# Attention values on four 64x64 array tiles, shared PSUM banks and a new instruction order in a fused attention and gated-MLP kernel

## The chip, the cores and the metric

The kernel runs on one core of one Trainium2 chip. The metric is the device time of one execution in microseconds; the median of several runs is compared, and a change is told from no change by runs of both kernels on the same chip. The core has five engines with queues of their own: TensorE (PE in the profile, with its weight loads as PEld), VectorE (DVE), ScalarE (ACT), GpSimd (POOL) and SyncE (SP, which here only issues DMAs). Every engine works off its own queue in order and waits on semaphores for the others.

## The reference

The input is an attention over short chunks, followed by a gated MLP. There are 4 batches, 8 heads, 768 positions and 64 dimensions a head.

```python
for c in range(nc):                       # 24 chunks of 32 queries
    l_start = max(0, c_start - 16); r_end = min(S, c_end + 8)
    k_full = concat([mem_k, k[l_start:r_end]])     # 8 + up to 56 keys = 64
    scores = scale * q_c @ k_full.T
    a = exp(scores - max(scores)); a = a / (sum(a) + 1e-9)
    out[c_start:c_end] = a @ v_full
x = out, heads side by side: (4, 768, 512)
h = gelu(x @ w_in); u, v = halves of h             # 512 and 512 wide
v_n = layer_norm(v) * g_ln
v_s = einsum('ts,bsd->btd', w_sg, v_n) + b_sg
y = x + (u * v_s) @ w_out
```

## The kernel before

The work is cut into 24 units `u` of 128 queries (4 batches `b`, 6 tiles `tt`), each with four chunks `c` and eight heads. A unit goes through these steps (`attention_steps`, L291), named with the unit's number:

- `q`, `k`, `v`: DMAs of the inputs, two, two and three buffers deep.
- `S`: 32 matmuls on tiles of 64 rows by 32 columns into two PSUM banks `s` (L159); the profile shows two records for each matmul in float32.
- `mx`, `sb`: DVE takes the largest score and subtracts it; `ex`: ACT's exponential; `z`: a few zeros by POOL; `sm`: DVE's sum, plus 1e-9, and reciprocal, three instructions in one step; `nm`: the product with it, on DVE or POOL.
- The weights must then lie with the keys on the partitions. Units 0 to 9 (`PAIRS = 10`) use TensorE: `T` transposes into the bank `t`, and `pa` and `pb` copy the two halves of partitions into `pt_all`. Units 10 to 23 use DVE and DMA: `yt` transposes blocks of 32x32, and `E`, once for two units, issues 16 DMAs of 32 KB from `y_t` to `pt_all`.
- `A`: the values (L382). Two heads share a matmul: 128 rows hold the keys of both heads, and `pt_all` keeps zeros in the other head's half, so that one matmul of 128 rows, 64 columns and 64 moving columns gives both. There are 16 matmuls, 32 records, into a bank `av` (L161).
- `xc`, `xh`, `xl`: copy of the result, its high part, and the low part (result minus high part), which the MLP multiplies as three products high x low, low x high and high x high.

The MLP is written in steps as well: `V` + batch + tile is the product for the gate half with 12 matmuls of 512 columns, followed by the gelu (`v1` to `v4`), the statistics (`v5`, three instructions), `v6` (POOL), `v7`, and `v8` and `v9` for the high and low parts. `U` + batch + half + block is the other half, with 12 matmuls of 384 columns, and `u1` to `u4`. `W` is the product over the sequence with 18 matmuls, and `w1` to `w4`; `O` is the last product with 12, `o1` adds the residual and `out` stores. The weights come as 64-bit floats and are taken apart by `d1` to `d9` (`weight_steps`, L199) and, for `w_sg`, by `ga` and `gb`; `cb` and `cbh` bring the two vectors. `zz6` stands for six warm matmuls of the identity that compute nothing needed. The products of the MLP and the warm matmuls write into a pool of four PSUM banks `mm` (L158); together with `s`, `t` and `av` all eight are taken.

What runs when is written out by hand: `ORDER` lists all steps in program order, and `InOrder` (L95) keeps each engine's instructions in that order. A step that can run on two engines has a star where the second one is taken (`nm0*` is on POOL, `d7i10*` on DVE). So the list is the queue of every engine, read by picking out its steps. Since every instruction passes through the helper `InOrder`, nearly all rows of the profile carry its line, L103, and are told apart by their tiles. Accesses to one PSUM tile by different engines are ordered bank by bank: an instruction that writes a bank waits for all earlier ones, in program order, that read that bank of the tile, and the other way round.

Of the kernel before, what the change touches and what calls it, by code (L numbers as in the profile page):

```python
# [39 lines left out]
d4i01 d5i00 d7i02* d2i03 d8i02 d1i03 d4i03 d2o0 d9i02* d3i03 nm1 d4o0 d5i03 T1 v100 d6o0 pa1 cbh v200 pb1  # L40
sb3 A1 v300 ex3 v400 T2 sm3 v4 xc1 d7i00 S4 pa2 v500 xh1 k6 nm3* pb2 mx4 q6 d8i00 A2 sb4 v600 ex4 S5 xl1* v5
xh2 T3 d9i00 sm4 q7 xc2 V01 k7 pa3 mx5 pb3 nm4 sb5 xl2 ex5 d6i03 S6 z5 v101 d6i01 A3 k8 mx6 q8 V02 d7i03* v6
xc3 v201 d8i03 d1i01 xh3 d9i03* v301 xl3* d3i01 v401 T4 V03 d5i01 pb4 v501 d7i01 pa4 sb6 v601 v700 d8i01 sm5
ex6 A4 v800 d9i01* z6 v701 S7 ga20 v7 nm5* sm6 ga50 U001 k9 ga41 mx7 xh4 q9 v900 ga00 xl4 v801 xc4 T5 gb20*
v103 U002 nm6 g11 pb5 gb00* pa5 v203 v901 g21 ga40 sb7 ga30 T6 v303 gb50* A5 ex7 gb40 v403 g10 pa6 sm7 S8
ga11 v8 gb41 xc5 V04 v503 g51 xh5 k10 gb11 mx8 ga21 q10 u1002 xl5 v603 g01 ga10 u2002 nm7* pb6 sb8 v102 A6
u3002 v202 gb10 ex8 u4002 S9 ga51 v9 sm8 gb30 xc6 U010 g31 v302 mx9 k11 gb51 u1001 q11 v402 ga01 u2001 gb01
v502 V05 u3001 u1010 v703 v602 u2010 v803 v702 u3010 gb21* v802 u4010 v903 ga31 T7 u4001 U012 pa7 pb7* v902
v105 sb9 v205 ex9 gb31 A7 v104 sm9 v305 v204 S10 u1012 v10 xc7 nm9 U003 k12 v304 v405 q12 u2012 mx10 u3012
v404 U000 u1003 u4012 v504 u2003 v604 U013 v505 u3003 u1000 u4003 v605 u2000 v704 u3000 U011 v705 v804 u4000  # L50
v805 v904* v905* d1o0 W002 nm8 d3o0 d5o0 ro1 d7o0 d8o0 T8 w1002 W003 d9o0 pa8 sb10 pb8* ex10 w2002 sm10
w3002 d1o1 d2o1 S11 d3o1 w4002* d4o1 W001 d5o1 k13 u1013 nm10 q13 d6o1 u2013 ro2 d7o1 mx11 u3013 w1003 A8
d8o1 u4013 w1001 W000 w2003 v11 xc8 w2001 w3003 d9o1* w3001 d2o2 d1o2 d4o2 w4001 d3o2 W013 d6o2 u1011 u2011
w4003 w1000 u3011 d5o2 w2000 ro3 d7o2 u4011 w3000 W012 w1013 d8o2 w4000* w2013 d9o2* w3013 w4013* d1o3 W010
d2o3 d3o3 w1012 d4o3 d5o3 w2012 d6o3 w3012 yt10 w4012 W011 w1010 d7o3 w2010 w3010 d8o3 w4010* d9o3 T9 w1011
pa9 sb11 O000 pb9 w2011 ex11 w3011 z11 sm11 O002 w4011* nm11* o1000 out000 O001 o1002 yt11 out002 O011 o1001
out001 O010 o1011 out011 O012 o1010 out010 O013 o1012 out012 O003 o1013 out013 S12 o1003 xh6 A9 xh7 out003
xl6* xh8 k14 mx12 V10 q14 xl7* E5 xl8* sb12 xc9 ex12 xh9 V12 z12 sm12 v110 xl9 v210 nm12* v310 v410 V11 v112
v510 v12 v212 v610 v312 v710 v412 v810 V13 v910 v512 yt12 v612 v111 v712 v211 v812 A10 v311 v912 U100 v411
v13 xc10 xh10 v511 v113 xl10 v213 A11 u1100 v611 v313 u2100 V14 v711 v14 xc11 v413 u3100 xh11 u4100 v811  # L60
v513 xl11 U101 v613 v911 v713 v114 V15 u1101 v214 v813 u2101 v314 v913 u3101 v414 u4101 U102 v514 v115 v215
v614 v714 v315 U103 v814 v415 u1102 v914 v515 u2102 v615 U110 u3102 u1103 v715 u4102 v815 u2103 v915 u3103
U111 u1110 u4103 u2110 u3110 u4110 W100 u1111 u2111 u3111 u4111 W101 w1100 w2100 w3100 w4100 W102 w1101
w2101 w3101 w4101 W103 w1102 w2102 w3102 w4102 U112 w1103 w2103 w3103 w4103 U113 u1112 u2112 u3112 u4112 S13
# [5 lines left out]
xl14 yt17 A15 o1112 out112 O113 xc15 E8 V20 o1113 xh15 xl15 V21 v120 v220 v18 out113 v320 v420 V22 v520 v121  # L70
v221 v620 v321 v720 v421 v820 A16 v920 v521 V23 v621 v19 xc16 v122 v721 xh16 v222 v821 xl16 v322 v422 A17
v921 v522 V24 v20 xc17 v622 v123 v722 xh17 v223 v822 xl17 v323 U200 v423 v922 v523 v124 v623 V25 v224 u1200
v723 v324 u2200 v823 v424 u3200 v923 v524 U201 u4200 v624 v125 v724 v225 v824 U202 v325 v924 u1201 v425
u2201 v525 u3201 U203 u1202 u4201 v625 u2202 v725 u3202 v825 u4202 U210 u1203 v925 u2203 u3203 u4203 W200
u1210 u2210 u3210 u4210 W201 w1200 w2200 w3200 w4200 W202 w1201 w2201 w3201 w4201 W203 w1202 w2202 w3202
w4202 U211 w1203 w2203 w3203 w4203 U212 u1211 u2211 u3211 u4211 S18 u1212 U213 u2212 k20 mx18 u3212 q20
u4212 sb18 W210 ex18 u1213 z18 sm18 u2213 nm18 u3213 u4213 S19 yt18 W211 w1210 k21 q21 mx19 w2210 sb19 w3210
w4210 ex19 sm19 W212 w1211 nm19 w2211 yt19 w3211 w4211 E9 S20 w1212 W213 w2212 mx20 w3212 w4212 sb20 ex20
sm20 S21 w1213 O200 nm20 mx21 k22 w2213 q22 sb21 w3213 k23 O201 q23 w4213 ex21 o1200 out200 sm21 nm21 A18
yt20 o1201 O202 v21 xc18 yt21 out201 A19 o1202 out202 O203 E10 xc19 S22 o1203 xh18 O210 xh19 xl18 mx22 sb22  # L80
xl19 ex22 S23 sm22 O211 out203 o1210 v22 mx23 out210 nm22 sb23 O212 o1211 ex23 out211 z23 yt22 sm23 A20
o1212 nm23 O213 out212 xc20 v23 yt23 xh20 xl20 A21 o1213 out213 V30 E11 xc21 xh21 xl21 V31 v130 v230 v330
v430 V32 v530 v131 v231 v630 v331 v730 v431 v830 V33 v930 v531 v631 v132 v731 v232 v831 A22 v332 v931 v432
U300 xc22 v532 v133 xh22 v233 v632 xl22 v333 A23 u1300 v433 U301 v732 xc23 v533 v832 xh23 u2300 v932 u3300
V34 u1301 u4300 xl23 u2301 u3301 v633 u4301 v733 V35 v833 v134 v933 v234 v334 v434 U302 v135 v534 v235 v634
v335 v734 U303 u1302 v435 v834 u2302 v934 v535 u3302 U310 u4302 u1303 v635 u2303 v735 u3303 v835 u4303 U311
u1310 v935 u2310 u3310 u4310 W300 u1311 u2311 u3311 u4311 W301 w1300 w2300 w3300 w4300 W302 w1301 w2301
w3301 w4301 W303 w1302 w2302 w3302 w4302 U312 w1303 w2303 w3303 w4303 U313 u1312 u2312 u3312 u4312 W310
u1313 u2313 u3313 u4313 W311 w1310 w2310 w3310 w4310 W312 w1311 w2311 w3311 w4311 W313 w1312 w2312 w3312
# [512 lines left out]
```

## Time and profile before

| | us |
|---|---|
| median of 3 runs | 420.61 |
| lowest, highest | 416.58, 421.05 |
| the profiled execution's own time | 422.26 |
| its span in the profile | 420.5 |

| engine | busy us | share of the span |
|---|---|---|
| PE | 378.9 | 90% |
| PEld | 346.8 | 82% |
| DVE | 283.5 | 67% |
| ACT | 166.8 | 40% |
| POOL | 130.2 | 31% |

The mean granted TensorE clock of the span is 0.971 of the full one. A busy engine is one that has an instruction in it. PE's matmuls are pipelined and their ends are modelled, so the time of a burst is best read from its first start to the next burst's first start. A row of the timeline gives start, length, engine, line, operation, tiles written and read, shape and count; a row of the waits gives total, count and longest.

### The profile page before, as it was taken

Reading aid. Unit: us, or ns where it says so; the run is one execution under the profiler, and the core shown is the slowest. Engines: PE = TensorE matmul, PEld = TensorE weight load, DVE = VectorE, ACT = ScalarE, POOL = GpSimd, SP = SyncE. Lnnn points to the kernel's source line nnn. Section 1 sums busy time; section 2 is a strip of 40 time slices with the busy share of each in tenths; the row PEclk is TensorE's granted clock in tenths of the full one; section 3 lists DMA queues with packets and bytes.
Section 4 is the critical chain, followed back from the end, with each engine's and each line's share of the span. In section 5 each row is a group of like instructions: output and inputs, shape, how many; then the busy total and the mean of one; then the engine's idle time right before and its main releaser. Section 6 shows DMA issues by size and latency. Waiting matters only on the chain. (4 is left out here: it accounts for less than half of the span.)

```text
span 420.5 us, 9642 instructions
## 1 busy us (share of the span) xinstructions
PE 378.9 (90%) x4026; PEld 346.8 (82%) x4026; DVE 283.5 (67%) x536; ACT 166.8 (40%) x307; POOL 130.2 (31%) x136
## 2 busy tenths in 40 slices
PE   3663998899989998999998979999989899999996
PEld 3652787699989977999986858999978888999996
DVE  5999799998994477845764555844973567753332
ACT  4545678654450236613222235623222246533100
POOL 3433346712331045421202225422111125422210
PEclk9996799999999999999999898999998999999999
DMA  8992656532412423001162924001227350000012
GB/s 289 397 388 94 223 161 206 195 112 82 133 50 76 142 89 107 2 0 63 36 222 55 320 71 146 2 0 62 64 50 246 101 160 21 2 0 2 0 64 88
DMA packets 24523, 47.56 MB, mean 113 GB/s; under 512 B 4384, under 2 KB 13600, under 8 KB 24480
## 3 DMA queue, kind: packets, MB, share of 16 engines
q1 hardware_dynamic: 24480, 46.94, 33.8%
q8 instruction: 32, 0.52, 0.5%
q14 instruction: 11, 0.09, 0.1%
HBM read 36.96 MB, written 6.29 MB: 103 GB/s over the span
## 5 line engine op out<-in xcount | busy, mean ns | idle before, releaser
L103 PE MATMUL s<-ka,qa 64*32 64x64 f32 x768 | 11.0, 238 | 8.1 <-DMA qa<-in_qs 5.7
L103 PEld LDWEIGHTS s<-ka,qa 64*32 64x32 f32 x768 | 9.0, 112 | 10.9 <-DMA ka<-in_ks 6.0
L103 PEld LDWEIGHTS av<-pt,vb 128*64 128x64 f32 x256 | 9.9, 156 | 7.8 <-issue 4.2
L103 PE MATMUL av<-pt,vb 128*64 128x64 f32 x256 | 11.5, 246 | 4.5 <-DMA pt<-y 2.4
L103 PEld LDWEIGHTS av<-pt,vc 128*64 128x64 f32 x256 | 9.2, 148 | 7.5 <-issue 5.9
L103 PE MATMUL av<-pt,vc 128*64 128x64 f32 x256 | 10.7, 237 | 4.9 <-DMA pt<-y 3.8
L103 ACT ACTIVATE eb<-eb 128x512 f32<-128x512 f32 x12 | 7.6, 630 | 18.2 <-DVE eb L103 17.8
L103 DVE STREAM_TRANSPOSE y<-ea 128x512 f32<-128x512 f32 x7 | 5.0, 710 | 13.6 <-DMA pt<-y 13.6
L103 PEld LDWEIGHTS av<-pt,va 128*64 128x64 f32 x256 | 8.4, 137 | 6.1 <-issue 3.9
L103 PE MATMUL av<-pt,va 128*64 128x64 f32 x256 | 9.7, 226 | 4.1 <-DMA pt<-y 2.9
L103 DVE SCALAR_TENSOR_TENSOR gb<-gb,mmd 128x512 f32<-128x512 f32 x12 | 8.2, 680 | 7.2 <-ACT gb L103 7.2
L103 ACT ACTIVATE ga<-ga 128x512 f32<-128x512 f32 (+1 forms) x14 | 8.8, 632 | 9.7 <-DVE ga L103 9.7
L103 ACT COPY pt<-t 64x512 f32<-64x512 f32 x18 | 10.4, 579 | 4.4 <-PE t L103 4.2
L103 PE MATMUL s<-kb,qb 64*32 64x64 f32 x768 | 10.7, 231 | 1.6 <-DVE ea L103 1.4
L103 PEld LDWEIGHTS s<-kb,qb 64*32 64x32 f32 x768 | 8.7, 109 | 3.9 <-DVE ea L103 1.8
L103 ACT COPY xa<-av 128x512 f32<-128x512 f32 x9 | 5.2, 583 | 16.1 <-PE av L103 14.1
L103 ACT ACTIVATE gb<-gb 128x512 f32<-128x512 f32 (+1 forms) x14 | 8.9, 635 | 5.8 <-DVE gb L103 5.7
L103 PE MATMUL mma<-ident 128*128 128x128 f32 x50 | 9.6, 356 | 1.4 <-POOL ident masks.py:199 1.4
L103 ACT ACTIVATE ea<-ea 128x512 f32<-128x512 f32 x12 | 7.6, 632 | 7.3 <-DVE ea L103 7.3
L103 DVE SCALAR_TENSOR_TENSOR gb<-gb,mmc 128x512 f32<-128x512 f32 x8 | 5.4, 678 | 7.4 <-ACT gb L103 7.4
L103 DVE SCALAR_TENSOR_TENSOR mma<-mma,g_half,b_half 128x384 f32<-128x384 f32 x9 | 5.5, 613 | 7.2 <-PE mma L103 7.2
L103 PEld LDWEIGHTS mma<-ident 128*128 128x128 f32 x50 | 8.5, 257 | 1.8 <-POOL ident masks.py:199 1.4
(501 smaller groups left out, 1286.8 us busy)
## 6 DMA issues: line engine op xcount, KB each, us to landing
ka<-in_ks SPq DMA_DIRECT2D x12, 368.0 KB, 3.9
kb<-in_ks SPq DMA_DIRECT2D x12, 368.0 KB, 5.3
va<-in_vs SPq DMA_DIRECT2D x8, 512.0 KB, 4.8
vb<-in_vs SPq DMA_DIRECT2D x8, 512.0 KB, 4.4
vc<-in_vs SPq DMA_DIRECT2D x8, 512.0 KB, 4.9
pt<-y SPq DMA_DIRECT2D x112, 32.0 KB, 1.9
qa<-in_qs SPq DMA_DIRECT2D x12, 256.0 KB, 4.5
qb<-in_qs SPq DMA_DIRECT2D x12, 256.0 KB, 5.2
```

What stands on the lines that cost most here:

```text
L103: return self.tc.keep_in_program_order(getattr(self.engine, name)(*args, **kw))
```

## The change

- **Values on four tiles.** `A` now issues one matmul for each head: 64 rows, 64 columns, 32 moving columns, 32 matmuls with 64 records in a unit. The two heads `h` use the two halves of the rows and write to two banks. `pt_all` holds no zeros, is half as large, and POOL no longer fills them at the start; one copy `p` of 128 partitions replaces `pa` and `pb`.
- **Two shared banks.** Scores take columns 0 to 255 and values columns 256 to 511 of the same two banks `sav`; the bank that `av` had goes to the pool `mm`, now five, and the pool of `u` buffers has seven instead of six. Since `sav` is one tile, `A` is ordered against `mx` and `sb`, and `S` against `xc`, `xh` and `xl` (the latter two where they read the bank, in units 0, 2, 4 and 5).
- **Small DVE operations split.** The three instructions of `sm` become the steps `sm`, `sa`, `sr`, and those of `v5` become `v5`, `vx`, `vy`, so that others can stand between them.
- **The exchange split.** `E` becomes four steps `Ea` to `Ed`, one for each chunk, with four DMAs each.
- **A new order,** with other choices of engine: on POOL instead of DVE are 17 `nm` (6 before); on DVE instead of POOL are 13 `v9` (2), 18 `w4` (5), 14 `xl` (9) and 7 `gb` (4); `d7` and `d9` change by one. Warm matmuls are 76 instead of 25, in eight places.

```diff
-N_U = 6
+N_U = 7
...
 ORDER = """
-ri10 ri00 ri12 g20 k0 q0 ri13 ri11 d1i10 q1 d2i10 d3i10 k1 zz6 d4i10 d5i10 ri01 d2i00 d6i10 d4i00 d2i12 ri02
...
-u1113 W110 u2113 q15 mx13 u3113 k15 u4113 sb13 ex13 sm13 W111 w1110 nm13 w2110 yt13 w3110 w4110 E6 W112
-w1111 w2111 w3111 w4111 S14 w1112 W113 w2112 mx14 w3112 w4112 sb14 k16 ex14 q16 sm14 S15 w1113 O100 nm14 k17
-mx15 q17 yt14 sb15 A12 w2113 ex15 o1100 w3113 O101 sm15 out100 xc12 w4113 v15 nm15 yt15 A13 o1101 out101
-O102 xc13 E7 O103 o1102 S16 o1103 xh12 O110 xh13 xl12 mx16 sb16 out102 xl13 out103 ex16 v16 S17 sm16 k18
-O111 q18 o1110 k19 mx17 q19 nm16 out110 sb17 A14 yt16 ex17 o1111 O112 z17 v17 xc14 sm17 out111 xh14 nm17
...
+ri10 k0 ri12 zz18 q0 ro0 v2 ri11 k1 g01 d1i10 d2i10 g31 d3i10 d4i10 d5i10 q1 d6i10 d1i12 ri00 d7i10* d3i12
+S0 d2i12 ri13 d8i10 zz19 d5i12 d4i12 d2o0 d9i10 mx0 k2 d4o0 sb0 d6o0 g21 ex0 d6i12 z0 d2i11 q2 d1i11 d4i11
...
+d6i01 xh0 zz6 k5 d7i13 mx3 q5 xl0 sb3 nm2* A1 d8i13 ex3 S4 v4 xc1 d9i13* T2 xh1 k6 d2i03 V00 d1i03 q6 d4i03
+xl1* p2 d2i02 d3i03 d6i03 d4i02 cbh sm3 mx4 V01 v100 sa3 sb4 sr3 v200 ex4 sm4 v300 v400 nm3* S5 v101 sa4
+v500 A2 d7i01 v201 q7 T3 k7 mx5 v301 zz6 v5 sr4 xc2 d7i00 vx00 v401 p3 vy00 sb5 xh2 v600 v501 d8i00 S6 nm4*
+ex5 xl2 d8i01 vx01 k8 mx6 A3 z5 q8 vy01 d9i01 sm5 T4 v6 xc3 V02 sa5 sr5 xh3 p4* d9i00 sb6 d6i02 v601 ex6
...
+vx12 vy12 v612 A10 v113 v712 V10 v213 v812 v13 xc10 v912 v313 xh10 v413 xl10 v513 A11 v110 vx13 vy13 S15
+v210 v613 Ec6 xc11 V14 v713 v310 mx15 xh11 v410 v813 xl11* q17 v913* k17 v510 V15 v114 Ed6 sb15 vx10 v214
+ex15 vy10 v314 sm15 v610 v414 Eb6 U111 v710 v514 v810 sa15 vx14 sr15 v910* U113 u1111 nm15* vy14 Ea6 v115
+u2111 v215 u3111 v614 u4111 v315 S16 v714 u1113 v415 U110 v814 v14 mx16 q18 v914 k18 v515 u2113 vx15 U112
+u3113 vy15 v615 yt14 u1110 v715 yt15 v815 sb16 A12 u1112 u4113 ex16 S17 u2110 v15 xc12 u2112 U103 u3110 k19
...
+w1102 w2102 w3102 w4102 O112 o1110 Eb7 W100 o1112 out110 out112 yt16 W103 w1100 yt17 w2100 sb18 w3100 w4100* ex18
+A14 w1103 z18 sm18 S19 v17 xc14 w2103 O111 sa18 k21 mx19 w3103 q21 sr18 w4103 sb19 ex19 nm18 O101 o1111 sm19
...
 """
...
-    pt_all = const.tile([P, 4, 2, 2, 4, CH], F32, name="pt")
+    pt_all = const.tile([P, 4, 2, 4, CH], F32, name="pt")
...
-    mms = Slots(buffers(4, [P, 512], F32, "mm", psum))
-    s_ps = psum.tile([P, 2, 512], F32, name="s")
+    mms = Slots(buffers(5, [P, 512], F32, "mm", psum))
+    sav_ps = psum.tile([P, 2, 512], F32, name="sav")
     t_ps = psum.tile([P, 512], F32, name="t")
-    av_ps = psum.tile([P, 4, P], F32, name="av")
+    s_v = sav_ps[:, :, 0:4 * KW].rearrange("p r (m k) -> p r m k", k=KW)
+    av_v = sav_ps[:, :, 4 * KW:512].rearrange("p h (a t) -> p h a t", a=2)
+    av_x = av_v.rearrange("p h a t -> p a h t")
...
-    for g in range(2):
-        gpsimd.memset(pt_all[64 * g:64 * g + 64, :, 1 - g], 0.0)
...
-        def total(eng):
-            eng.tensor_reduce(rd, e, axis=AX.X, op=ALU.add)
-            eng.tensor_scalar_add(rd, rd, 1e-9)
-            eng.reciprocal(rd, rd)
...
-        step(f"sm{u}", total, vector)
+        step(f"sm{u}", lambda eng: eng.tensor_reduce(rd, e, axis=AX.X, op=ALU.add), vector)
+        step(f"sa{u}", lambda eng: eng.tensor_scalar_add(rd, rd, 1e-9), vector)
+        step(f"sr{u}", lambda eng: eng.reciprocal(rd, rd), vector)
...
-            def part(h):
-                def does(eng):
-                    f = eng.copy if eng is scalar else eng.tensor_copy
-                    f(pt_all[64 * h:64 * h + 64, :, h, j], t_v[64 * h:64 * h + 64])
-                return does
+            def place(eng):
+                f = eng.copy if eng is scalar else eng.tensor_copy
+                f(pt_all[:, :, j], t_v)
...
-            def exchange(eng):
-                for c in range(4):
+            def exchange(c):
+                def does(eng):
                     for h in range(2):
                         for b_ in range(2):
                             at = 64 * h + 32 * b_
                             eng.dma_start(
-                                pt_all[at:at + 32, c, h], y_t[32 * c:32 * c + 32, h, b_]
+                                pt_all[at:at + 32, c], y_t[32 * c:32 * c + 32, h, b_]
                             )
+                return does
...
-                        eng.matmul(
-                            av_ps[64 * r:64 * r + 64, 2 * a:2 * a + 2, CH * c:CH * c + CH],
-                            v[:, c, r, a], pt_all[:, c, :, j, 2 * r + a], start=True, stop=True,
-                        )
+                        for h in range(2):
+                            rows = slice(64 * h, 64 * h + 64)
+                            eng.matmul(
+                                av_v[64 * r:64 * r + 64, h, a, CH * c:CH * c + CH],
+                                v[rows, c, r, a], pt_all[rows, c, j, 2 * r + a], start=True, stop=True,
+                            )
+
+        def by_pair(x):
+            return x[:, :, sl].rearrange("p (a h) t -> p a h t", h=2)
...
-        step(f"xc{u}", lambda eng: eng.copy(x32[:, :, sl], av_ps), scalar)
+        step(f"xc{u}", lambda eng: eng.copy(by_pair(x32), av_x), scalar)
...
-        def stats(eng):
-            eng.bn_stats(st, gs.held[key])
-            eng.bn_aggr(mv, st)
-            eng.tensor_scalar_add(rs, mv[:, 1:2], 4.0 * LN_EPS)
...
+        step("v5" + n, lambda eng: eng.bn_stats(st, gs.held[key]), vector)
+        step("vx" + n, lambda eng: eng.bn_aggr(mv, st), vector)
+        step("vy" + n, lambda eng: eng.tensor_scalar_add(rs, mv[:, 1:2], 4.0 * LN_EPS), vector)
```

More of the change, by code (lines that the diff above doesn't have):

```diff
@@ L40 @@
[L40 to L64, printed above, removed]
@@ L70 @@
[L70 to L89, printed above, removed]
@@ new lines @@
+vy02 sm9 U001 gb31* v602 g11 sa9 gb20* g00 v702 g30 sr9 v904* v802 U002 nm9 v105 gb10* ga11 v205 v902 g51
+ga00 A7 v305 gb21* ga30 S10 gb11 v405 v103 g40 T8 v10 xc7 v203 gb00 k12 u1010 U003 v505 v303 q12 u2010 gb30
+ga51 vx05 u1001 v403 u3010 gb51 vy05 u2001 u1002 U013 u4010 ga40 v605 v503 u3001 u1003 v705 u4001 v805 U000
+vx03 u2003 vy03 v905* u3003 v603 mx10 v703 U012 u4003 v803 sb10 v903 u2002 ex10 p8* u3002 U011 sm10 u4002
+sa10 d1o0 sr10 gb40* d3o0 T9 gb50* u1012 A8 d5o0 u1011 p9 W001 nm10* u2012 ro1 xc8 u2011 v11 u3012 u3011
@@ new lines @@
+gb41* d7o0 u4012 u1013 u4011 u2013 d8o0 W012 w1001 u3013 d2o1 u4013 d4o1 d1o1 w2001 d3o1 d6o1 w3001 d5o1
+W002 w1012 w4001 ro2 w2012 d7o1 u1000 w3012 u2000 u3000 d9o0* d8o1 W000 u4000 w4012 w1002 d9o1 w2002 w3002
+d1o2 d2o2 d3o2 w4002 W003 d4o2 w1000 d5o2 d6o2 w2000 ro3 d7o2* w3000 w4000* d8o2 W010 w1003 d9o2* w2003
+w3003 d1o3 w4003* S11 d3o3 d2o3 w1010 W013 d4o3 q13 mx11 k13 w2010 d6o3 w3010 d5o3 sb11 w4010 A9 yt10 ex11
+d7o3* S12 z11 v12 w1013 d8o3 W011 sm11 q14 d9o3* k14 sa11 w2013 sr11 mx12 w3013 nm11* sb12 O003 w1011 w4013
@@ new lines @@
+out111 sa19 sr19 nm19* O100 o1101 out101 O102 o1100 out100 A15 o1102 S20 out102 Eb8 O103 mx20 O113 q22 o1103
+xh14 Ea8 xh12 xl14* xh13 xl12 V22 o1113 xl13* out113 v18 Ed8 V20 v122 v222 v322 Ec8 v422 U200 v522 v120 vx22
+v220 out103 vy22 v320 v622 k22 U203 v420 u1200 u2200 v520 u3200 yt18 V21 u1203 u4200 xc15 sb20 xh15 yt19
+ex20 xl15 u2203 vx20 sm20 u3203 A16 u4203 sa20 vy20 V23 v722 v620 v19 xc16 sr20 nm20* v822 xh16 v922* xl16*
+v121 A17 v720 v221 V24 v820 Ea9 xc17 v920* v321 v123 v421 xh17 v223 xl17 v521 v323 U202 Ed9 vx21 v423 vy21
@@ new lines @@
+v523 v621 V25 v721 u1202 vx23 Ec9 v821 vy23 u2202 v623 u3202 v921 u4202 v723 v124 U211 Eb9 v823 v224 v923*
+v324 v125 v424 U212 u1211 v225 v20 u2211 v325 v524 u3211 v425 U213 u1212 u4211 v525 yt20 A18 vx25 u2212
+u1213 vx24 vy25 u3212 u2213 S21 v625 vy24 v21 xc18 u4212 v624 U201 u3213 mx21 q23 k23 u4213 v725 sb21 v825
+A19 v724 u1201 ex21 v925 S22 u2201 v22 xc19 sm21 U210 v824 mx22 u3201 v924* u4201 sa21 W212 sb22 sr21 ex22
+nm21 sm22 yt21 sa22 Ec10 sr22 nm22* W210 w1212 w2212 w3212 w4212 Ed10 u1210 W201 w1210 u2210 u3210 Ea10
@@ new lines @@
+u4210 w2210 w3210 W202 w1201 w4210* Eb10 w2201 w3201 w4201* W203 w1202 w2202 w3202 w4202* yt22 A20 w1203
+W213 w2203 v23 xc20 w3203 w4203* A21 w1213 W200 w2213 w3213 w4213 W211 w1200 w2200 w3200 w4200 O201 w1211
+w2211 w3211 w4211* S23 o1201 O213 out201 mx23 sb23 ex23 O210 o1213 z23 sm23 out213 sa23 sr23 nm23 O211 o1210
+yt23 out210 Ed11 O200 o1211 Eb11 O202 o1200 O203 o1202 out200 Ea11 O212 o1203 xh19 xh20 xl19 out203 xh18
+Ec11 xl20* V31 o1212 xl18 out212 out211 V32 out202 v131 v231 v331 v431 U301 v531 v132 xc21 vx31 v232 xh21
@@ L374, in exchange @@
                             eng.dma_start(
-                                pt_all[at:at + 32, c, h], y_t[32 * c:32 * c + 32, h, b_]
+                                pt_all[at:at + 32, c], y_t[32 * c:32 * c + 32, h, b_]
                             )
+                return does
             step(f"yt{u}", blocks, vector)
             if j:
-                step(f"E{u // 2}", exchange, sync)
+                for c in range(4):
+                    step(f"E{'abcd'[c]}{u // 2}", exchange(c), sync)
         def values(eng):
```

51 lines of the change are left out of this document (38 added, 13 removed).

## The prediction

> **What bounds the kernel now.** I read the page's head and DVE's slices, then a table of the span by stages, the waits of PE, the chain that ended last, and single bursts on PE.
>
> ```profile
> span 420.5 us, 9642 instructions
> DVE  5999799998994477845764555844973567753332
> ```
>
> DVE's slices (busy tenths, 10.5 us each) say two kernels: in the first nine, to 95 us, it is full, later hardly ever. The stage table (length, then busy time with instructions of PE, PEld, DVE, ACT, POOL, then granted clock, DMA share, GB/s) gives sizes:
>
> ```profile
> 0.00:48.00 48.00, 26.34 (x557) 22.33 (x558) 40.12 (x70) 26.12 (x42) 18.84 (x23) 0.86 0.77 282
> 48.00:95.00 47.00, 43.82 (x656) 37.88 (x654) 45.55 (x89) 32.92 (x65) 20.98 (x22) 1.00 0.54 174
> 206.00:257.00 51.00, 45.07 (x539) 38.80 (x538) 28.85 (x57) 13.77 (x24) 12.70 (x13) 0.93 0.51 161
> 257.00:312.00 55.00, 55.00 (x554) 52.52 (x551) 37.97 (x75) 20.91 (x40) 16.46 (x17) 1.00 0.13 40
> 312.00:351.00 39.00, 34.93 (x413) 29.98 (x412) 21.13 (x41) 10.88 (x18) 8.76 (x9) 0.96 0.49 147
> ```
>
> PE is short of work in the first row and nearly full in the second, where DVE is busy 45.55 of 47. From 257 to 312 PE has no gap and full clock; from 206 to 257 and from 312 to 351 it has gaps and a lower clock. The waits of PE and the chain name the cause:
>
> ```profile
> PE av L103 <- DMA pt<-y: 9.2, 7, 2.2
> ```
> ```profile
> 303.62 0.51 SPq L103
> ...
> 315.76 0.24 issue
> ...
> 340.93 2.80 PE mma L103 x12
> ...
> 362.50 2.09 PE mmc L103 x12
> ...
> 370.83 3.12 PE mmc L103 x18
> ```
>
> One exchange (16 issues on SP from 303.62 on, then the last landing, at 315.76, where PE goes on) takes 12.1 us, and the values of its units stand behind it. What this costs is seen when the six bursts A12, A14, A16, A18, A20, A22 are cut out from their first matmul to the next product (PE busy with av alone, clock, DMA):
>
> ```profile
> 211.91:213.96 2.05, 1.30 (x32) 1.00 0.38 88
> 228.12:232.20 4.08, 1.51 (x32) 0.99 0.32 97
> ...
> 349.26:351.18 1.92, 1.30 (x32) 1.00 0.14 34
> sum 18.07, PE 8.25; mean PE 1.38
> ```
> ```profile
> 142.20 0.86 PE L103 MATMUL s<-ka,qa 64*32 64x64 f32 x64
> 142.99 1.15 PE L103 MATMUL av<-pt,va 128*64 128x64 f32 x32
> 144.07 1.20 PE L103 MATMUL mmc<-w_in_hi,paira 128*128 128x512 f32 x4
> ```
>
> An undisturbed burst takes 144.07 - 142.99 = 1.08, so the six lose 18.07 - 6.48 = 11.6 us. After three of them the next work runs at a low clock (all of PE):
>
> ```profile
> 232.20:236.02 3.82, 3.82 (x15) 0.56 0.90 286
> 251.71:256.24 4.53, 4.53 (x15) 0.62 0.75 257
> 316.38:319.62 3.24, 3.24 (x15) 0.67 0.92 262
> ```
>
> That is 3.82 x 0.44 + 4.53 x 0.38 + 3.24 x 0.33 = 4.5 us more. The exchange costs 16.1 us in all.
>
> **The change, part by part.**
>
> *Exchange.* Its 16 issues and 12.1 us stay. What decides is the PE work that the order puts between the moment it may start and the values. Per step PE needs S 0.79 (142.20 to 142.99), A 1.08, V 2.80, U and O 2.09, W 3.12 (chain rows). The start needs the block transposes yt of both units and the values of the pair before, which read the same pt. Between these and the next values the old list has 9.9, 11.0, 11.6, 8.9, 11.0 and 12.3 us for A12 to A22, so all but the last stand under 12.1 even if DVE and SP are never late, and A22 shows 0.8 of loss. The new list has 15.5, 16.6, 17.5, 13.9, 12.5 and 20.9 (and 30.8 for A10). Between the four pieces stand at most some k, q, v and out issues, under 0.8 us each (12.1 / 16); of those that themselves wait, out113 sits between two pieces of E8 and out103 before its last, and 17.5 covers them. A20 alone is tight, 1 us left. Gain 16.1 - 1.0 = 15.1. Ends: 8 (queues late by some us each) to 16.1.
>
> *Order and engine choices before the first W.* DVE's queue sets PE here, so I add what the list puts on DVE ahead of a product and subtract the PE work ahead of it. One 512-wide instruction takes 0.61 from start to start, and 384-wide ones three quarters of that:
>
> ```profile
> 21.30 0.68 DVE L103 SCALAR_TENSOR_TENSOR md<-rawd,md 128x512 f32<-128x512 uint32 x1
> 21.91 0.69 DVE L103 SCALAR_TENSOR_TENSOR exb<-rawb,exb 128x512 int32<-128x512 int32 x1
> ```
>
> Old list, first W (W002): DVE 76.9, PE 54.3, difference 22.6 (the stage table's 85.7 busy less the 10.9 of blocking below is 74.8, so the sum is about right). New list, first W (W001): 8 fewer 512-wide (nm 4, d9 2, d7 1, xl 1) and 6 more (p 2, sb, d5, v9 and one reduction), 4 fewer u and 2 more gb of 384, tiny operations that no longer stand behind their producer, about 0.1 each (estimate: the 0.08 by which rows overlap): DVE 73.7, PE 56.2, difference 17.5. The new list's worst product is V04 with 41.8 - 22.8 = 19.0. Gain 22.6 - 19.0 = 3.6.
>
> Against it stands POOL, which gets 17 nm for 6 and 36 tensor operations ahead of the first W for 31. Beside a POOL operation some DVE rows are long:
>
> ```profile
> 10.11 1.50 DVE L103 TENSOR_SCALAR me<-rawe 128x512 int32<-128x512 int32 x1
> ...
> 17.35 1.77 DVE L103 SCALAR_TENSOR_TENSOR mb<-rawb,mb 128x512 f32<-128x512 uint32 x1
> ...
> 80.35 1.63 DVE L103 TENSOR_TENSOR w_sg_lo<-uf,w_sg_hi 128x384 fp32r<-128x384 f32 x1
> ```
> ```profile
> 17.30 1.27 POOL L103 TENSOR_TENSOR w_in_lo<-mc,w_in_hi 128x512 fp32r<-128x512 f32 x1
> ```
>
> Fifteen such rows, the first at 10.11 and the last at 80.35, hold 10.9 us over their kinds' medians, a third of a us for each of 31 POOL operations. Five more cost 1.7 us; ends 0 (they meet no such row) and 5 (each blocks a full one). The Trainium skill, SBUF — State Buffer, section "Who interferes with whom", speaks against this part: a VectorE instruction with two SBUF inputs contends with a GpSimd one that reads SBUF, and whoever issued first holds the shared port to its end. By that rule alone all five block and the stage gains nothing; the rows at 17.30 and 17.35 show such a pair, but not every pair meets. Net gain taken: 1.9.
>
> *Values by 64x64 tiles.* Each unit now has 64 matmul records of 32 columns instead of 32 of 64, on four tiles instead of two: 16 turns on each tile, as before. A turn can be set by the moving columns, which halve, or by the weight load, which keeps 64 columns:
>
> ```profile
> L103 PEld LDWEIGHTS mmc<-w_in_hi,paira 128*128 128x128 f32 x8 | 1.4, 188 | 0.3
> ...
> L103 PEld LDWEIGHTS av<-pt,va 128*64 128x64 f32 x32 | 1.0, 138 | 0.1
> ```
>
> 64 columns more cost 50 ns, so by these rows (an estimate) 64 columns cost some 50 ns themselves: most of a turn today (1.08 / 16 = 67 ns with lead-in), whatever the moving side does. I take no gain: 1.08 stays. Ends: half of it, a gain of 0.54 x 24 = 13.0; and each record at its present 34 ns, a loss of 1.08 x 24 = 25.9. S, with 64 records in 0.79 (though on smaller tiles with half the load), speaks against 34 ns as the price of a record, so the loss is the far end.
>
> *Scores and values in the same two banks.* A must now wait for mx and sb of the scores before it, and the next S for xc, xh, xl, wherever the list has them in between. From u = 7 on the list has 2 us or more of products there, or lets S follow A at once and the reader after. Bare are A1 behind sb3, S6 behind sb5 and A3 behind mx6, some 1.4 us each (two 512-wide instructions of 0.69): PE stands there, but DVE is the bound and keeps other work queued (xl, d steps). Nothing; up to 4 us if DVE then lacks scores, and below nothing excluded, since a wait is added and none taken.
>
> *The rest,* one answer each. The zero fill leaves POOL's first microseconds, before any weight has come: nothing. One 128-partition copy replaces two of 64, ten instructions fewer on ACT, which is busy 26.12 of 48 us: nothing; were ACT the bound, 10 x 26.12 / 42 = 6 us. The copies out of av read the same 512 columns: nothing. A fifth mm bank and seventh u buffer ease PE's waits for DVE there, under 2 us, within the DVE-bound stage: nothing. The 51 more warm matmuls need 19.6 us at the price of the present 25, of the 21.7 in which PE idles in the first stage:
>
> ```profile
> L103 PE MATMUL mma<-ident 128*128 128x128 f32 x50 | 9.6, 356 | 1.4 <-POOL ident masks.py:199 1.4
> ```
>
> Nothing; without cover S1, behind 19 of them, comes some us later. The loads are reordered on SP, but DVE's first weight piece is first in both lists; the sixth and seventh transfers move up (v2, ri11), about 3.2 MB at 282 GB/s or 11 us, when DVE's sum reaches d2i11: nothing, and if late DVE stands for that long.
>
> Sum: -15.1 - 1.9 = -17.0. Against the profiled execution, 420.5 + 1.8 around it = 422.3, that is 405.3; the median shown is 420.6, 1.7 under the profiled one, so 403.6.
>
> **The rivals.**
> - *Streamed columns set a turn.* Values halve: 403.6 - 13.0 = 390.6. For it: four tiles exist, and S runs eight. Against: the load rows. The Trainium skill, TensorEngine Tiling (Array Packing), section "Theoretical Speedup", gives up to 2x for a contraction of 64 or less; by it the sum would be this rival's.
> - *The exchange wait stays.* Reads of scores come late through the shared banks, the pieces stand in SP's queue behind an out that waits, and the 15.1 come back: 418.7. For it: SP is in order and the list gives A20 no slack. Against: 13.9 to 20.9 us elsewhere.
> - *The start loses.* Every unit up to S10 shows its bank wait to DVE: 11 x 1.4 = 15 us, 418.6 or some part of it. Against: DVE has other work there.
> - *Slower: a record keeps its 34 ns.* Values take 2.16 in each unit, 403.6 + 25.9 = 429.5. It decides from a burst of about 1.08 + 21.2 / 24 = 1.96 us on (17.0 gained, and 1% more). For it: the extra 768 matmuls and loads are real. Against: S, unless its shorter load is what makes it quick.
>
> **How the numbers follow.** Forecast 0.62, columns 0.12, exchange 0.08, start 0.10, records 0.08. About 1% (4.2 us) can be told from no change here. Faster: 0.62 + 0.12 + half of the start's 0.10 = 0.79; same: 0.08 + 0.05 = 0.13; slower 0.08. The forecast's own ends are 396 (exchange 16.1, DVE 3.6, values a third of the way to half) to 412 (exchange 8, banks and POOL some us each). The range 389 to 414 takes in the columns' case and leaves out 0.21.
>
> **What would show it.** Right: no DMA pt<-y among PE's long waits, clock 1.00 after 130 us, the first W some 2 us earlier against the PE work done, A bursts of 1.0 to 1.1 us with 64 records. Wrong: A at 0.6 or at 2; PE waiting for eb, mx or xc readers before A and S; long DVE rows beside nm on POOL making the first W later than 95 us.

## The result and the profile after

The changed kernel takes 404.62 us (median of 4 runs, 403.0 to 405.58); the kernel before took 420.09 beside it (416.58 to 421.05). The ratio is 0.964, with an interval from 0.958 to 0.971. Forecast were 403.6 and a range of 389 to 414.

The head of the page after, with the slices of PE, DVE and the granted clock:

```profile
span 403.8 us, 11335 instructions
...
PE   7788788999989999999999999998999999999996
...
DVE  4996889999989567897637358895636456756532
...
PEclk9996999999999999999999999999999999999999
```

PE is full from the eighth slice on, with dents in slices 12 and 28, and the clock is low in one slice only, the fourth. The stage table of the kernel after, in the stretches shown of before:

```profile
0.00:48.00 48.00, 38.18 (x764) 34.39 (x764) 37.19 (x71) 24.45 (x41) 17.08 (x23) 0.93 0.83 303
48.00:95.00 47.00, 41.66 (x811) 36.96 (x812) 43.81 (x86) 28.60 (x57) 26.19 (x27) 1.00 0.47 154
206.00:257.00 51.00, 51.00 (x620) 46.88 (x620) 32.36 (x64) 16.92 (x31) 10.82 (x12) 1.00 0.39 121
257.00:312.00 55.00, 52.78 (x704) 50.43 (x703) 36.08 (x74) 17.70 (x34) 8.59 (x10) 1.00 0.23 73
312.00:351.00 39.00, 38.87 (x313) 34.70 (x312) 23.88 (x48) 17.09 (x32) 10.34 (x10) 1.00 0.14 45
```

The two stages in which the exchange left PE idle, 206 to 257 and 312 to 351, are filled, 51.00 and 38.87 us of work at full clock (45.07 at 0.93 and 34.93 at 0.96 before). A new loss of 2.2 us stands in the stage that had none, 257 to 312. The waits of PE after:

```profile
PE sav L109 <- issue: 2.3, 2, 1.5
PE sav L109 <- DVE eb L109: 2.0, 1, 2.0
PE sav L109 <- DVE ea L109: 2.0, 2, 1.3
PE sav L109 <- DVE exb L109: 1.9, 1, 1.9
PE sav L109 <- ACT w_in_hi L109: 1.6, 1, 1.6
```

No line names pt<-y any more. Ahead stand waits of the shared banks (sav) for VectorE, and one for nothing that the profile shows ("issue"). The exchange that the forecast called tight, that of units 20 and 21, in the timelines of SP and PE (start, length):

```profile
279.72 10.01 SPq L109 DMA_DIRECT2D pt<-y  x16
```
```profile
292.33 1.15 PE L109 MATMUL sav<-pt,vc 64*64 64x32 f32 x64
```

Its last issue ends at 289.73. A20 starts 2.6 us later without an idle time before it, so it did not wait.

To place gains and losses I use the lag of PE: the start of one of its steps, less the PE work listed before it at the prices of the prediction (S 0.79, A 1.08, T 0.44, V 2.80, U and O 2.08, W 3.12; warming matmuls count nothing). It is worked out from the starts in the traces. Rows are PE work done, in us, and a row stands for the first step with at least that much work ahead of it; the columns are the experiments below, in short:

```
done  before  after | no exch. shared old ord. | old banks joinedE tiny  few warm nm DVE
                    | (e1)     (e12)  (e3)     | (e9)      (e4)    (e6)  (e7)     (e11)
  10    34.3   30.0 |   32.2    34.8    34.6   |   26.4     30.2   29.0   35.2    29.0
  20    35.8   34.5 |   32.5    38.3    38.3   |   28.7     34.7   35.6   41.8    34.8
  35    38.0   38.4 |   34.7    44.1    43.9   |   33.2     38.6   39.2   45.4    39.5
  60    41.2   40.2 |   37.9    46.4    48.1   |   46.2     40.5   40.9   47.4    41.7
 160    46.2   45.2 |   42.3    50.8    54.1   |   48.5     46.0   48.3   51.0    47.0
 200    58.1   45.7 |   44.0    63.3    70.4   |   49.0     48.7   48.9   51.7    47.6
 230    58.2   49.0 |   44.1    63.4    70.5   |   49.7     52.6   55.7   53.9    52.5
 290    67.0   50.4 |   46.4    71.1    80.3   |   51.1     54.4   57.2   55.3    54.1
```

From 160 to 290 the kernel before lost 20.8 us and the changed one 5.2: 15.6 of the 16.6 us that lie between them at 290 come from there. Of the start's gain little is left: 0.7 at the first W (lag 40.8 before, 40.1 after) and 1.0 at 60.

### The profile page after: what moved, and what is told of

The parts are those of the page before. It is cut to its first block, busy times and chain, and to the rows that moved or that the text cites. A ratio compares the mean times of both kernels' runs of the same rounds, so it can differ in the third digit from the quotient of the medians.

```text
span 403.8 us, 11335 instructions
## 1 busy us (share of the span) xinstructions
PE 379.8 (94%) x4896; PEld 353.5 (88%) x4896; DVE 285.8 (71%) x558; ACT 160.8 (40%) x296; POOL 104.4 (26%) x113
## 4 chain that ended last, share of the span: by engine, by line
PE 69%; DVE 19%; DMA 4%; issue 3%; ACT 3%; POOL 1%; SPq 0%; DVEq 0%; POOLq 0%; ACTq 0%
PE mmc L109 13%; PE mma L109 13%; PE mmd L109 12%; PE mmb L109 11%; PE mme L109 11%; PE sav L109 8%; DVE ga L109 2%; DMA y<-in_w_out 2%; DVE gb L109 2%; DMA rawc<-in_w_in 2%; DVE xo L109 1%; DVE rdb L109 1%; DVE w_sg_lo L109 1%; DVE eb L109 1%; ACT ga L109 1%
## 5 line engine op out<-in xcount | busy, mean ns | idle before, releaser
L109 PE MATMUL mma<-ident 128*128 128x128 f32 x136 | 18.3, 295 | 1.4 <-POOL mhalf L109 1.4
L109 PEld LDWEIGHTS mma<-ident 128*128 128x128 f32 x136 | 17.2, 208 | 1.7 <-POOL mhalf L109 1.4
L109 PE MATMUL sav<-pt,va 64*64 64x32 f32 x512 | 9.4, 221 | 6.4 <-DVE eb L109 2.0
L109 PE MATMUL sav<-ka,qa 64*32 64x64 f32 x768 | 10.8, 231 | 4.3 <-DMA qa<-in_qs 1.5
L109 PEld LDWEIGHTS sav<-ka,qa 64*32 64x32 f32 x768 | 8.7, 109 | 6.2 <-issue 4.2
L109 PEld LDWEIGHTS sav<-pt,vb 64*64 64x64 f32 x512 | 9.1, 143 | 5.5 <-ACT w_in_hi L109 1.8
L109 PE MATMUL sav<-pt,vb 64*64 64x32 f32 x512 | 10.1, 228 | 3.1 <-ACT w_in_hi L109 1.6
L109 PE MATMUL sav<-kb,qb 64*32 64x64 f32 x768 | 10.3, 224 | 1.9 <-DVE exb L109 1.9
L109 ACT COPY xa<-sav 128x512 f32<-128x512 f32 x9 | 5.2, 583 | 13.6 <-PE sav L109 10.9
L109 PE MATMUL mma<-w_in_hi,paira 128*128 128x512 f32 x32 | 9.9, 435 | 0.0
L109 PE MATMUL sav<-pt,vc 64*64 64x32 f32 x512 | 9.2, 221 | 0.0
```

The costliest lines, as they stand in the source:

```text
L109: return self.tc.keep_in_program_order(getattr(self.engine, name)(*args, **kw))
```

## The experiments

All times stand beside runs of the kernel before on the same chip (medians 420.3 to 421.3).

### The exchange taken out of both kernels (e1, e2)

Edit of the kernel before; the same in the changed kernel:

```diff
             def exchange(eng):
-                for c in range(4):
+                for c in range(0):
                     for h in range(2):
```

> Left out: the kernel before without the transfers of the exchange (units 10 to 23 multiply the probabilities that unit 8 and 9 left in pt). Everything else, its order included, stays. Theory A (the forecast): the exchange is the wait that the change removes, 15.1 us of it, so this kernel is 14 to 17 us below the kernel before, 404 to 406 us. Rival (the changed kernel's gain is in its matmuls and banks, not in the exchange): the wait is only handed on to the next link of the same chain and this kernel gains less than 8 us, 412 us or more.

> Left out: the changed kernel without the transfers of the exchange. Theory A: they are already hidden behind other TensorE work; 0 to 1.5 us below the changed kernel, 403 to 405 us. Rival (the exchange is only partly hidden, its end near 8 us of the forecast's 16 still stands in the changed kernel): 6 us or more below it.

Measured: e1 402.05 us (ratio 0.960, 0.953 to 0.968), e2 404.49 (0.965, 0.957 to 0.974). The stage table of e1:

```profile
206.00:257.00 51.00, 51.00 (x535) 45.16 (x535) 35.31 (x72) 21.38 (x38) 18.84 (x19) 1.00 0.41 132
...
312.00:351.00 39.00, 39.00 (x300) 34.28 (x298) 25.63 (x54) 20.18 (x37) 16.24 (x17) 1.00 0.09 30
```

The same two stages fill up as in the changed kernel. The exchange cost the kernel before 18.3 us by the medians; in the trace 20.8 - 4.1 = 16.7 from 160 to 290. (At 35 us of work, before the first exchange, e1's lag is already 3.3 smaller, which its transfers cannot have caused.) In the changed kernel its removal brings 0.1, with an interval of some 3.6 us to either side: the theory, that the exchange is hidden whole, fits, and the rival's 6 us or more do not.

### Two orders by two sets of mechanisms (e3, e9)

e3 puts the old order into the changed kernel. e9 puts the old banks, values and copies under the new order:

```diff
-    mms = Slots(buffers(5, [P, 512], F32, "mm", psum))
+    mms = Slots(buffers(4, [P, 512], F32, "mm", psum))
...
-    sav_ps = psum.tile([P, 2, 512], F32, name="sav")
+    s_ps = psum.tile([P, 2, 512], F32, name="s")
+    av_x = psum.tile([P, 4, P], F32, name="av")
...
-                        for h in range(2):
-                            rows = slice(64 * h, 64 * h + 64)
...
+                        eng.matmul(
+                            av_x[64 * r:64 * r + 64, 2 * a:2 * a + 2, CH * c:CH * c + CH],
+                            v[:, c, r, a], pt_all[:, c, :, j, 2 * r + a], start=True, stop=True,
+                        )
```

For want of room e9 keeps the exponents of w_out in the third x buffer, which units 6 to 8 overwrite; so its products with w_out are of other numbers, in the same instructions.

> The changed kernel with the order of the kernel before (25 warming matmuls with it): 64x64 tiles, five matmul buffers, shared banks, one copy out of the transposes, transfers of the exchange in four steps one behind the other at the old place. Theory A: without the new order nothing of the gain is left, 417 to 424 us (nothing from tiles and tiny operations, 0 to 4 us lost to the shared banks, where the old order puts scores just ahead of values). Rival (streamed columns set the time of the values): 24 units lose half of 1.08 us each, 13 us, 407 us.

> The new order with the old mechanisms: scores and values in banks of their own, four matmul buffers, block-diagonal values (32 matmuls, two copies out of the transposes, zeros filled at the start); eight steps of TensorE stand a little later in the text, so that a buffer is free for each. With the run of the changed kernel in the old order (435.5 us) this fills the table of two orders by two mechanisms. Theory A now (the shared banks cost waits, 15 us of them in the old order, and the new order only hides them): without them the new order does at least as well, 396 to 404 us. Rival (the fifth buffer and the tiles are part of the gain, and the new order needs them): 409 us or more.

```
                  old order       new order
old mechanisms    420.1           405.3 (ratio 0.963, 0.958 to 0.969)
new mechanisms    435.5 (1.039)   404.6 (ratio 0.964, 0.958 to 0.971)
```

The interval of e3 is 1.033 to 1.045. Neither of e3's forecasts comes near: in the old order the new mechanisms cost 15 us. For e9 the time falls between both forecasts, and its trace says why. The lag is 5.8 us *smaller* than in the changed kernel at 20 us of work, where scores and values no longer wait for each other's readers. In the changed kernel A1, S6 and A3 wait there, in its timeline of PE:

```profile
31.39 0.42 PE L109 MATMUL sav<-pt,vb 64*64 64x32 f32 x12 [1.63 <-ACT w_in_hi L109]
...
48.11 0.86 PE L109 MATMUL sav<-ka,qa 64*32 64x64 f32 x64 [1.13 <-ACT paira L109]
50.48 1.14 PE L109 MATMUL sav<-pt,va 64*64 64x32 f32 x64 [1.52 <-DVE rsb L109]
```

In e9 A1 waits 0.81 us, A3 0.46, and S6 does not wait. In the changed kernel VectorE stands too, at xl2, which reads the values of unit 2 in a bank that S6 writes before it:

```profile
49.07 0.69 DVE L109 TENSOR_TENSOR paira<-sav,paira 128x512 fp32r<-128x512 f32 x1 [1.04 <-PE sav L109]
```

At 60 us of work the lag of e9 is 6.0 us larger. In between, PE stands at U002; the waits and the timeline of e9:

```profile
PE mmb L106 <- DVE gb L106: 5.2, 1, 5.2
```
```profile
71.74 1.55 PE L106 MATMUL mmc<-paira,w_in_hi 128*128 128x384 f32 x8
78.47 1.65 PE L106 MATMUL mmb<-paira,w_in_lo 128*128 128x384 f32 x4 [5.18 <-DVE gb L106]
```

U002 writes mmb, and VectorE has not yet finished with what stands there: with four matmul buffers none is free. This one wait takes the whole lead: U002 starts at a lag of 38.5 us in e9 and of 38.4 in the changed kernel. So the shared banks cost some 5 us at the start, and the fifth buffer, which is what the sharing buys, pays them back before the first W. The other 6 us that e9 falls behind have several sources that were not separated: waits of 0.95, 0.84 and 1.81 us at U003, U011 and W001, a clock of 0.91 and 0.93 granted from 66 to 84 and from 84 to 107 us (1.00 in the changed kernel from 66 to 100), and 2.1 us of second copies on VectorE.

Behind the first W it turns again. From 60 to 290 the changed kernel loses 10.2 us of lag and e9 4.9: the changed kernel waits 2.01 us before A9, 0.70 before A12, 0.73 before A19 and 1.49 within S22, and e9 waits at none of them. So under the new order the two sets of mechanisms end level. (e9 has the old form of the values too, and two copies for one; e5 below shows the form to be worth nothing. The eight steps that stand later are those that lack a buffer, with what follows them on PE.)

### Sharing alone (e12)

The kernel before, with its values moved into the upper halves of the banks of the scores:

```diff
-    av_ps = psum.tile([P, 4, P], F32, name="av")
+    av_ps = s_ps[:, :, 4 * KW:512].rearrange("p a (h t) -> p a h t", h=2)
...
-                            av_ps[64 * r:64 * r + 64, 2 * a:2 * a + 2, CH * c:CH * c + CH],
+                            av_ps[64 * r:64 * r + 64, a, :, CH * c:CH * c + CH],
```

> The kernel before with one edit: its values go to the upper halves of the two banks of the scores (their own bank stays unused; four matmul buffers, block-diagonal values and the order as before). Theory A (the changed kernel in the old order lost 15 us to the shared banks): 430 to 437 us, with sav-like waits of A and S for VectorE's sb and ScalarE's xc, up to 8 us of them before the first W. Rival (tiles, the joined copy or the split steps lost them): within 3 us of the kernel before.

Measured: 427.03 us, ratio 1.016 (1.005 to 1.027), between theory and rival: 6 us. The waits of PE that are new in it (that of `t` for eb is smaller, 4.0 for 6.5):

```profile
PE s L103 <- DVE eb L103: 3.6, 3, 2.6
PE s L103 <- DVE paira L103: 2.9, 1, 2.9
```

Its lag is 6.1 us above that of the kernel before at 35 and no more than that later (4.1 at 290). VectorE's idle time shows the same: of the time up to the first W its instructions cover 86.1 us before and 86.5 in e12, and it has none for 9.0 us before and 13.9 in e12. The other 9 of e3's 15 us are not isolated. In e3's trace they stand mostly in the stages of the exchange (54.1 to 80.3, 5.4 more than before), and one stop within S9 of 1.74 us is of the kind shown below.

### The values: what sets a turn (e5, e8)

e5 takes the old form in units 10 to 23 of the changed kernel (the zeros filled behind unit 9):

```diff
+                        if u >= PAIRS:
+                            eng.matmul(
+                                av_ah[64 * r:64 * r + 64, a, :, CH * c:CH * c + CH],
+                                v[:, c, r, a], pt_all[:, :, c, j, 2 * r + a], start=True, stop=True,
+                            )
+                            continue
```

e8 varies one size at a time, from unit 10 on:

```diff
+                            form = u % 4 if u >= PAIRS else 0
+                            wide = 32 if form == 1 else 64
+                            cols = 16 if form == 2 else CH
+                            ab = slice(0, 2) if form == 3 else slice(a, a + 1)
```

> The changed kernel with the old form of the values in units 10 to 23 (32 matmuls of a 128x64 stationary tile and 64 moving columns, half of them zeros, in place of 64 matmuls of a 64x64 tile and 32 columns); two fills on GpSimd behind unit 9 make the zeros. Theory A (a turn is set by the load of the weights, which is the same in both): bursts of 1.0 to 1.1 us as in both kernels, time within 1 us of the changed kernel. Rival (streamed columns): the old form takes 0.54 us longer in each of 14 units, 7.6 us more. Rival (a fixed price of each matmul): the new form costs more, and this kernel is 5 us or more faster.

> Changed computation: from unit 10 on the values take four forms by the unit's number modulo 4: 0 as in the changed kernel (64x64 stationary, 32 moving columns), 1 with 32 columns of weights (64x32), 2 with 16 moving columns, 3 with 64 moving columns, each 64 matmuls. Read from the trace, the time between the first start and the last of each burst. Theory A (the load of 64 weight columns sets the turn): form 0 near 1.05 us, form 1 near half of it, form 2 unchanged, form 3 unchanged or a little longer. Rival (moving columns set it): form 1 unchanged, form 2 near half, form 3 near double. Rival (a fixed price of each matmul): all four the same.

Measured: e5 403.74 us (0.961, 0.955 to 0.966), 0.9 below the changed kernel, within what can be told, with S22 whole (271.23 us on, 0.86 long). One undisturbed burst of each form in the timeline of e8 (stationary tile, then moving columns; the length reaches to the modelled end of the last matmul):

```profile
290.76 1.15 PE L109 MATMUL sav<-pt,vc 64*64 64x32 f32 x64
...
295.21 0.76 PE L109 MATMUL sav<-pt,va 64*32 64x32 f32 x64
...
333.05 1.12 PE L109 MATMUL sav<-pt,vb 64*64 64x16 f32 x64
...
336.40 1.16 PE L109 MATMUL sav<-pt,vc 64*64 64x64 f32 x64
```

With 16, 32 or 64 moving columns the burst is 1.12, 1.15 and 1.16; with half the columns of weights it is 0.76. From the first start to the last the trace has 0.92, 0.93 and 0.94 against 0.56 to 0.62, and 0.93 for the old form. The columns of the weights set the turn, the moving columns do not; the forecast's "nothing" holds for the reason that it gave. The Trainium skill, TensorEngine Tiling (Array Packing), section "Theoretical Speedup", allows up to 2x for a dimension of 64; for this shape the runs show none.

### The split steps and the warming matmuls (e4, e6, e7)

Each undoes one edit in the changed kernel's order: e4 joins the four pieces of each exchange, e6 the tiny operations (sm then does sum, add and reciprocal, v5 both statistics and the add), e7 leaves 16 of 76 warming matmuls.

```diff
-w2011 Ec5 sm12 w3011 O000 o1003 w4011 sa12 sr12 nm12 out003 O011 Ed5 o1000 S13 o1011 Ea5 O013
+w2011 Ea5 Eb5 Ec5 Ed5 sm12 w3011 O000 o1003 w4011 sa12 sr12 nm12 out003 O011 o1000 S13 o1011 O013
...
-sm1 d3i13 g50 S2 sa1 p0 sr1
+sm1 d3i13 g50 S2 p0
...
-zz18 ... zz19 ... zz11 ... zz6 ... zz8 ... zz6 ... zz6 ... zz2
+zz4 ... zz4 ... zz2 ... zz1 ... zz2 ... zz1 ... zz1 ... zz1
```

> The changed kernel with the four steps of each exchange joined again at the place of the first, so that all 16 transfers are issued in one row. Theory A: it is the distance between the exchange and its values, not the split, that hides it; within 2 us of the changed kernel. Rival (the split is what lets other transfers of the queue pass between): 4 us or more above it, with q, k or out seen late.

> The changed kernel with the tiny VectorE operations (sum, add, reciprocal of the softmax; statistics, their sum, add of the normalisation) again one behind the other at the place of the first. Theory A: the pauses between them are short and VectorE is not the bound after the start; 0 to 2 us slower. Rival (their split is a main term): 4 us or more slower.

> The changed kernel with 16 warming matmuls instead of 76, at the same places. Theory A: 0 to 2 us slower; a lower granted clock in the first 35 us, which VectorE and the transfers bound. Rival (the clock of the start is what made the start faster): 3 us or more slower. Second rival: the warming matmuls stand in the way, and without them it is 1 us or more faster.

Measured: e4 408.94 us (0.977, 0.970 to 0.983), e6 410.78 (0.977, 0.971 to 0.983), e7 411.98 (0.980, 0.975 to 0.985); 4.3, 6.2 and 7.4 us above the changed kernel. In all three the rival was nearer than the theory. The changed kernel's interval ends at 0.971, so e7 lies clear of it, while e4 and e6 begin where it ends.

*e4.* From 160 to 200 the lag grows by 2.7 us (0.5 in the changed kernel), and before A16 PE then waits 1.95. The queue of SP after, and with the pieces joined:

```profile
228.97 3.10 SPq L109 DMA_DIRECT2D pt<-y  x4
232.16 0.54 SPq L109 DMA_DIRECT2D qa<-in_qs  x1
```
```profile
229.97 11.68 SPq L106 DMA_DIRECT2D pt<-y  x16
241.75 0.53 SPq L106 DMA_DIRECT2D qa<-in_qs  x1
242.37 0.38 SPq L106 DMA_DIRECT2D out<-xa  x1
242.81 0.42 SPq L106 DMA_DIRECT2D va<-in_vs  x1
243.28 0.48 SPq L106 DMA_DIRECT2D out<-xc  x1
```

Four transfers (qa to out) now start together. The last of them, an output, lands 5.0 us after its issue (2.1 in the changed kernel, where it starts at 242.31) and holds the x buffer until then; in e4's timelines of ACT, DVE and PE the rest of the chain follows:

```profile
248.27 0.58 ACT L106 COPY xc<-sav 128x512 f32<-128x512 f32 x1 [2.83 <-DMA out<-xc]
```
```profile
248.88 0.69 DVE L106 TENSOR_TENSOR ea<-sav,mxc 128x512 f32<-128x512 f32 x1 [3.17 <-ACT xc L106]
```
```profile
249.63 1.62 PE L106 MATMUL sav<-pt,vb 64*64 64x32 f32 x64 [1.95 <-DVE ea L106]
```

*e6.* Three statistics operations joined, and split, in the timelines of DVE:

```profile
269.50 0.69 DVE L102 BATCH_NORM_STATS2 stc<-ga 128x6 f32<-128x512 f32 x1
270.22 0.18 DVE L102 BATCH_NORM_AGGREGATE mvc<-stc 128x2 f32<-128x6 f32 x1
270.44 0.15 DVE L102 TENSOR_SCALAR rsc<-mvc 128x1 f32<-128x1 f32 x1
```
```profile
266.53 0.17 DVE L109 BATCH_NORM_AGGREGATE mvb<-stb 128x2 f32<-128x6 f32 x1
266.61 0.12 DVE L109 TENSOR_SCALAR rsc<-mvc 128x1 f32<-128x1 f32 x1
266.65 0.54 DVE L109 SCALAR_TENSOR_TENSOR ub<-ub,mma 128x384 f32<-128x384 f32 x1
```

Joined, they start 0.72 and 0.22 us apart, each behind the end of its producer; split, 0.08 and 0.04, inside one another. VectorE has 96 such operations. PE's waits before A12 and A19, for readers of the scores in the shared bank, are 1.86 and 2.27 us (0.70 and 0.73 in the changed kernel). From 160 to 230 the lag grows by 7.4 against 3.8; a lower clock in that stage (0.94 granted from 257 to 312, against 1.00) is part of it.

*e7.* The transposes of unit 0 and the scores of unit 3 in the timeline of PE, with few warming matmuls:

```profile
20.11 1.12 PE L106 MATMUL t<-ident,ea 128*128 128x128 f32 x4 [2.42 <-POOL ea L106]
...
28.31 1.13 PE L106 MATMUL sav<-kb,qb 64*32 64x64 f32 x58
32.84 0.43 PE L106 MATMUL sav<-kb,qb 64*32 64x64 f32 x6 [3.40 <-issue]
```

and in the changed kernel:

```profile
19.97 0.66 PE L109 MATMUL t<-ident,ea 128*128 128x128 f32 x4 [0.52 <-POOL ea L109]
...
27.36 0.86 PE L109 MATMUL sav<-kb,qb 64*32 64x64 f32 x64
```

Two things are lost. Bursts run slow (T 1.12 for 0.66), as at half clock; in e7's trace the first record of a granted clock stands at 43.8 us, in the changed kernel's at 4.7 (the view's clock column has nothing else to go by until then). And S3 is cut by 3.40 us with nothing to wait for, and A1 and S4 behind it stand for 2.42 and 0.99. How the 7.4 us divide between them was not tried.

### The place of the multiplications, and four mended places (e11, e10)

```diff
-... nm1* ... nm2* ... nm4* ... nm6* ... nm8* ... nm10*
+... nm1 ... nm2 ... nm4 ... nm6 ... nm8 ... nm10
```

> The changed kernel with six multiplications of the probabilities (nm of units 1, 2, 4, 6, 8 and 10) back on VectorE, where the kernel before had them. By the forecast's terms VectorE has 6 x 0.61 = 3.7 us more to do ahead of the first W and GpSimd blocks it 6 x 0.33 = 2 us less: 1 to 4 us slower. Rival (VectorE does not set the start any more): within 1 us of the changed kernel. Rival (GpSimd's blocking costs more than the instructions it takes over): 1 us or more faster.

Measured: 407.28 us (404.49 to 409.71), ratio 0.966 (0.957 to 0.975): 2.7 above the changed kernel, within the forecast's 1 to 4, but not to be told from it by the interval. At 60 its lag is 1.5 larger.

```diff
-A19 v724 u1201 ex21 v925 S22 u2201 v22 xc19 sm21 U210
+A19 v724 u1201 ex21 v925 u2201 v22 xc19 sm21 U210 S22
-S11 d3o3 d2o3 w1010 W013 ... sb11 w4010 A9
+S11 w1010 W013 ... sb11 d1o3 d3o3 d2o3 w4010 A9
-yt14 u1110 v715 yt15 v815 sb16 A12
+yt14 sb16 u1110 v715 yt15 v815 A12
-mx21 q23 k23 u4213 v725 sb21 v825 A19
+mx21 sb21 q23 k23 u4213 v725 v825 A19
```

> The changed kernel with four places of its order mended: S22 behind U210, so that no 256 short matmuls and loads stand in a row there; sb11 ahead of the last piece of w_out; sb16 ahead of v715 and yt15; sb21 right behind mx21. Theory (the stop of 1.5 us within S22 is the fetch of the next 256 instructions, and A9, A12 and A19 wait for the reader of the scores in the shared bank): 1.7 + 0.7 + 0.9 + 1.0, some 3 to 5 us less than the changed kernel, 400 to 402 us, no issue stop within S22. Rival (these waits only move to the next product): within 1.5 us of the changed kernel.

Measured: 403.92 us (0.960, 0.954 to 0.965), 0.7 below the changed kernel, the rival's size. The stop within S22 is gone, and so are the waits before A9, A12 and A19; V11 now waits 1.11 us and W212 0.55. The changed kernel, then e10, in the timeline of PE:

```profile
271.95 0.76 PE L109 MATMUL sav<-ka,qa 64*32 64x64 f32 x53
274.19 0.33 PE L109 MATMUL sav<-ka,qa 64*32 64x64 f32 x11 [1.49 <-issue]
```
```profile
272.31 0.86 PE L106 MATMUL sav<-ka,qa 64*32 64x64 f32 x64
```

Its profiled execution is 2.4 us shorter (span 401.4). The medians do not show that much, so it is no proven gain over the changed kernel.

## Why the prediction was right, point by point

*Exchange, -15.1: right.* 15.6 in the lag, and e1 and e2 show the cause; in e1's trace the whole wait is 16.7, and 16.1 were counted. One count was uneven: for A14, A16, A20 and A22 the old list's figures include the burst of the pair before (1.08), and the new list's do not. Counted alike, the old list has 9.9, 9.9, 10.5, 8.9, 9.9 and 11.2, all under 12.1, which only strengthens the step. That the pieces need only stand far ahead was too simple: joined they are as far ahead, and cost 4.3 (e4), because other transfers then start late.

*Order and engine choices before the first W, -1.9: -0.7, by other terms.* The work was counted well. VectorE's busy time up to the first W fell from 86.1 to 82.5 us (3.6; 3.2 counted), and GpSimd's price of 1.7 did not come: 13 long VectorE rows hold 10.8 us over their kinds' medians, where 15 held 10.9. But VectorE's idle time rose from 9.0 to 13.9, for which the sum had no term, and sharing the banks alone raises it as much (e12). The first W started at 96.4 us, behind the 95 that was named as a sign of being wrong (95.1 before, with 2.0 us less PE work ahead of it). The -0.7 is the balance of larger sums: the shared banks (+5.8 at 20 us of work), the fifth buffer (some -5, the wait at U002 in e9), the warming matmuls (-7 by e7). These do not add up to -0.7: the rest of the new order must cost some 6 us there, which no run isolates. Six multiplications put back on VectorE cost 2.7 (e11), which fits the forecast and does not prove it.

*Values, 0: right*, for the reason given (e8): an undisturbed burst takes 1.06 to 1.08 us from its first start to the next product's, 1.08 before. What the forecast overlooked are the 768 more matmuls and as many loads as instructions to be fetched: the stop in S22 (1.49) is gone in e5, which has the old form there.

*Shared banks, 0 (up to 4): the step that failed.* The three bare places waited as named and by the size named (A1 1.63, S6 1.13, A3 1.52, for 1.4 each), and the sign of being wrong, PE waiting for eb before A and S, was there. I held that VectorE had other work while PE stood. But VectorE's later work needs those scores and, as xl2 shows, that bank: the wait costs 6.0 in the old order (e12) and 5.8 at the start of the new one (e9). That nothing is bare from unit 7 on was wrong as well: A9, A12 and A19 wait 3.4 us together.

*Fifth buffer, 0, and warming matmuls, 0: failed*, in the other direction. I had priced both as cover for waits in the trace of before. The buffer pays for the shared banks at the start; the warming matmuls are worth 7.4 in this order.

*Split steps: too small.* The forecast gave 0.1 us to each tiny operation ahead of the first W and nothing to the rest. Joined they cost 6.2 (e6), 0.7 of it by 60 us of work.

So the time was right by its largest term. That it came within 1 us is luck: a second set of terms cancels, and taken alone each was mis-sized by 5 us or more. The rivals fell: columns by e8, the exchange by e2, a dear record by e5 and e8; the start lost part of what its rival said and had it back.
